# Splitting the last 64 contraction rows of the attention output into row-tiled pairs, and preparing their operand early

## The chip, the cores and the metric

One core of one Trainium2 chip runs the whole kernel. The metric is device time in microseconds (us) of one execution. Most executions of one kernel agree within 0.3%. From 2% a change is called faster or slower; what is compared are ratios with their 95% intervals.

## The reference, cut to what matters

```python
x = A_x                       # 2048 tokens x 576, bfloat16
xn = _layernorm(x, axis=-1)
return x + _A_ref(xn, A_wqkv, A_wo) + _B_ref(xn, B_w_gate, B_w_up, B_w_down)

# _A_ref: linear attention with H = 32 heads of 18 channels
#   o = num / den  (pq times kv per head, over pq times z), then o @ wo
# _B_ref: (gelu(xn @ w_gate) * (xn @ w_up)) @ w_down, F = 4608
```

The kernel folds kv (per head) and wo into one matrix M of 576 rows, so the attention output is (pq / den) @ M: a contraction over 576 rows, added to the same PSUM accumulator as the down projection, a contraction over 4608 rows.

## The kernel before

Four stages alike work on 512 tokens each. In each, 18 blocks of gate/up run on row tiles: two matmuls of 64 contraction rows at once, one in each half of the array. Then the down projection runs on the full array: per tile of 128 tokens and per column half of 288, 36 passes for the down weights and 5 for the attention part. The 32 heads are packed by 7, 7, 7, 7 and 4, so that four chunks have 126 rows and the last has 72:

```python
HCH = [7, 7, 7, 7, 4]                  # heads per chunk; DH = 18
...
    def m_stage(c, acc_bank):          # M = kv @ wo, chunk by chunk, while the first down tile runs
        rows = DH * HCH[c]
        for hf in range(2):
            b = (acc_bank + 2 + (2 * c + hf) % 6) % 8
            hs = slice(hf * HALF, (hf + 1) * HALF)
            nc.tensor.matmul(ps_all[:rows, b, :HALF], lhsT=kvT[:rows, c, :rows], rhs=wo2[:rows, c, hs], ...)
            nc.scalar.copy(out=m_sb[:rows, c, hs], in_=ps_all[:rows, b, :HALF])
...
            for f in range(NF):                    # 36 passes
                nc.tensor.matmul(acc, lhsT=hT[:, f, ...], rhs=wd_sb[:, f, hs], start=(f == 0), stop=False)
            for c in range(NCH):                   # 5 passes
                rows = DH * HCH[c]
                nc.tensor.matmul(acc, lhsT=pqT[:rows, c, ts_], rhs=m_sb[:rows, c, hs], ..., stop=(c == NCH - 1))
```

All loads of these stages are issued by SyncE, one after the other and in program order. In the first stage this one list holds the gate/up weights (three blocks ahead of use), the down weights (12 slices at blocks 2 to 13) and the transposed stores of pq / den.

```python
            if blk > 0:
                load_gu(blk + NWBUF - 1, i)        # four issues a block
...
        if sc == 0 and k == 1:
            load_wo()
        elif sc == 0 and k >= 2:
            load_wd_slice()
...
            if den_jobs and 0 < k < NF // GUB - 1:
                job, n = den_jobs.pop(0)           # every fourth of these issues a transposing store
                job(n)
```

Of the kernel before, what the change touches and what calls it, by code (L numbers as in the profile page):

```python
# [9 lines left out]
ALU = mybir.AluOpType  # L10
BF16 = mybir.dt.bfloat16
# [4 lines left out]
P = 128  # L16
HP = 64
S = 2048
D = 576
H = 32  # L20
DH = 18
F = 4608
NS = S // P
NF = F // P
SC = 512
NSC = S // SC
TPC = SC // P
HALF = D // 2
KT = 5
HCH = [7, 7, 7, 7, 4]  # L30
HOFF = [0, 7, 14, 21, 28]
NCH = len(HCH)
CR = 7 * DH
# [24 lines left out]
def kernel(  # L58
# [11 lines left out]
    nc = tc.nc  # L70
# [5 lines left out]
    out_view = out.flatten_outer_dims().rearrange("(p n) d -> p n d", n=NS)  # L76
# [5 lines left out]
    fwork = ctx.enter_context(tc.tile_pool(name="fwork", bufs=3))  # L82
    psum = ctx.enter_context(tc.tile_pool(name="psum", bufs=1, space=PSUM))

    ps_all = psum.tile([P, 8, 512], F32, name="ps_all")
# [4 lines left out]
    x_sb = persist.tile([P, NS, D], BF16, name="x_sb")  # L90
# [46 lines left out]
    pqT = persist.tile([P, NCH, S], BF16, name="pqT")  # L137
# [5 lines left out]
    hT = h_store[:].rearrange("p (f t) -> p f t", f=NF)  # L143
# [8 lines left out]
    def load_gu(i, part):  # L152

        if i >= NSC * NF // GUB:
            return
        f0 = GUB * (i % (NF // GUB))
        c0, c1 = f0 * P, (f0 + GUB) * P
        if part == 0:
            gu_blocks[i] = (wg_bufs.next(), wu_bufs.next(), wr_bufs.next())
        wg, wu, wr = gu_blocks[i]  # L160
        if part == 0:
            nc.sync.dma_start(wg[:], B_w_gate[0:512, c0:c1].rearrange("(kt p) c -> p kt c", p=P))
            nc.sync.dma_start(wr[0:HP, :], B_w_gate[512:576, c0:c1])
        else:
            nc.sync.dma_start(wu[:], B_w_up[0:512, c0:c1].rearrange("(kt p) c -> p kt c", p=P))
            nc.sync.dma_start(wr[HP:P, :], B_w_up[512:576, c0:c1])
# [13 lines left out]
        out=bm3, in_=bm3, compare_op=ALU.is_ge, fill=0.0,  # L180
# [3 lines left out]
        out=bm3, in_=bm3, compare_op=ALU.is_ge, fill=0.0,  # L184
# [109 lines left out]
    LO, HI = slice(0, HP), slice(HP, P)  # L294
    SYNC = mybir.DependencyInfo(mybir.DependencyClass.Sync, mybir.DependencyReason.DATA)
    banks = _Ring([4, 5, 6, 7, 2, 3, 0, 1])

    class _Unit:
# [5 lines left out]
        def __init__(self, outs, lhs, rhs, relay, first=(4, 0, 1, 2, 3), then=(0, 1, 2, 3)):  # L304
            self.outs, self.lhs, self.rhs, self.relay = outs, lhs, rhs, relay
            self.first, self.then = first, then
# [55 lines left out]
    def heads(ap):  # L362
        return ap.rearrange("p (h e) -> p h e", e=DH)
# [14 lines left out]

    def den_scale(n):
        pn = den_pn[n] = pn_bufs.next()  # L380
        for c0, c1 in ((0, 4), (4, 5)):
            h0, h1 = HOFF[c0], HOFF[c1 - 1] + HCH[c1 - 1]
            nh = HCH[c0]

            def chunked(ap):
                return ap.rearrange("p (c h) e -> p c h e", h=nh)

            nc.vector.scalar_tensor_tensor(  # L388
                out=pn[:].rearrange("p (c t) -> p c t", t=P)[:, c0:c1, :nh * DH].rearrange("p c (h e) -> p c h e", e=DH),
                in0=chunked(heads(pq[:, n, h0 * DH:h1 * DH])), scalar=EPS_ATT,  # L390
                in1=chunked(den_d[n][:, h0:h1].unsqueeze(2).to_broadcast([P, h1 - h0, DH])),
                op0=ALU.add, op1=ALU.mult,
            )

    def den_transpose(n):
        nc.sync.dma_start_transpose(pqT[:, :, n * P:(n + 1) * P], den_pn[n][:])
# [20 lines left out]
    for n in range(NS):  # L417
# [7 lines left out]
        if n < TD:  # L425
            for i, (k0, k1, eng) in enumerate([(0, 3, "ACT"), (3, KT, "ACT" if n else "DVE")]):
                b = TP_BANK[n] - i
# [98 lines left out]
    wd_sb = wd_pool.tile([P, NF, D], BF16, name="wd_sb")  # L526
    wo2 = wd_pool.tile([P, NCH, D], BF16, name="wo2")
    m_sb = wd_pool.tile([P, NCH, D], BF16, name="m_sb")
    dwork = ctx.enter_context(tc.tile_pool(name="dwork", bufs=1))
    pn_bufs = _Ring([dwork.tile([P, NCH * P], BF16, name=f"pn{i}") for i in range(3)])  # L530
    for pn in pn_bufs.tiles:
        nc.gpsimd.memset(pn[:], 0.0)

    def load_wo():
        nc.sync.dma_start(wo2[:CR, 0:4, :], A_wo[0:4 * CR, :].rearrange("(c p) j -> p c j", p=CR))
        nc.sync.dma_start(wo2[:D - 4 * CR, 4, :], A_wo[4 * CR:D, :])
    wd_loaded = [0]

    def load_wd_slice():
        f0 = wd_loaded[0]  # L540
        if f0 < NF:
            nc.sync.dma_start(wd_sb[:, f0:f0 + WDS, :], wd_view[:, f0:f0 + WDS, :])
            wd_loaded[0] += WDS


    den_jobs = [(job, n) for n in range(NS) for job in (den_mul, den_inv, den_scale, den_transpose)]

    def gu_pair(sc, k):
        cs = slice(sc * SC, (sc + 1) * SC)
        blk = sc * (NF // GUB) + k  # L550
        wg, wu, wr = gu_blocks.pop(blk)
        units = []
        for i in range(GUB):
            b = [banks.next(), banks.next()]
            fcol = slice(i * P, (i + 1) * P)

            def lhs(a, rows, kt, fcol=fcol):
                if kt == 4:
                    return wr[rows, fcol]
                return (wg, wu)[a][rows, kt, fcol]  # L560

            u = _Unit([ps_all[:, b[0], :], ps_all[:, b[1], :]], lhs, lambda a, rows, kt: xnT[rows, kt, cs],
                      nc.sync if blk == 0 else nc.gpsimd)
            if blk > 0:
                load_gu(blk + NWBUF - 1, i)
            u.p1()
            units.append((b, u))
# [4 lines that stand above are left out]
        for i, (b, u) in enumerate(units):  # L572
            u.p2()
            gl = fwork.tile([P, SC], F32, name="gl")
            nc.scalar.activation(out=gl[:], in_=ps_all[:, b[0], :], func=ACT.Gelu_apprx_tanh)  # L575
            nc.vector.tensor_tensor(out=hT[:, GUB * k + i, :], in0=ps_all[:, b[1], :], in1=gl[:], op=ALU.mult)  # L576
            if den_jobs and 0 < k < NF // GUB - 1:
                job, n = den_jobs.pop(0)
                job(n)

    def m_stage(c, acc_bank):
        rows = DH * HCH[c]
        for hf in range(2):
            b = (acc_bank + 2 + (2 * c + hf) % 6) % 8
            hs = slice(hf * HALF, (hf + 1) * HALF)
            nc.tensor.matmul(  # L586
                ps_all[:rows, b, :HALF], lhsT=kvT[:rows, c, :rows], rhs=wo2[:rows, c, hs], start=True, stop=True,
            )
            nc.scalar.copy(out=m_sb[:rows, c, hs], in_=ps_all[:rows, b, :HALF])

    def down_tile(sc, j, hooks):
        n = sc * TPC + j
        ts_ = slice(n * P, (n + 1) * P)
        res = fwork.tile([P, D], BF16, name="res")
        last = n == NS - 1
        for hf in range(2):
            hs = slice(hf * HALF, (hf + 1) * HALF)
            todo = hooks.pop(0) if hooks else {}
            acc_bank = banks.next()
            acc = ps_all[:, acc_bank, :HALF]  # L600
            for f in range(NF):
                if f in todo:
                    todo[f](acc_bank)
                nc.tensor.matmul(  # L604
                    acc, lhsT=hT[:, f, j * P:(j + 1) * P], rhs=wd_sb[:, f, hs], start=(f == 0), stop=False,
                )
            for c in range(NCH):
                rows = DH * HCH[c]
                nc.tensor.matmul(  # L609
                    acc, lhsT=pqT[:rows, c, ts_], rhs=m_sb[:rows, c, hs], start=False, stop=(c == NCH - 1),  # L610
                )
            nc.vector.tensor_tensor(out=res[:, hs], in0=acc, in1=x_sb[:, n, hs], op=ALU.add)  # L612
            if last:
                nc.sync.dma_start(out_view[:, n, hs], res[:, hs])
        if not last:
            nc.sync.dma_start(out_view[:, n, :], res[:])

    for sc in range(NSC):
        for k in range(NF // GUB):
            gu_pair(sc, k)  # L620
        while wd_loaded[0] < NF:
            load_wd_slice()

        hooks = [{6 * c_: (lambda b, c_=c_: m_stage(c_, b)) for c_ in range(NCH)} if sc == 0 else {}]
        for j in range(TPC):
            down_tile(sc, j, hooks)


# [28 lines left out]
```

## Time and profile before

| | before |
|---|---|
| median of 3 runs, at first | 516.69 us |
| span of the profiled run | 514.5 us |
| TensorE busy | 509.2 us, 99% |
| one full pass of 288 columns | 122.5 ns from start to start |
| one pair of row tiles, 512 columns | 215.9 ns |
| share of the DMA engines, first gate/up stage | 1.02 |

The lines are in the prediction. PE is TensorE, PEld its loads of stationary operands, DVE VectorE, ACT ScalarE and SPq the queue of SyncE; L309 is line 309 of the kernel. L309 is gate/up, L604 (after the change L632) a pass over the down weights, L609 (L637) a pass of the attention part, L586 (L589) the product that makes M; the new pairs are L620. In the page's groups, the text after the last bar is the idle time of the engine before these instructions, with who ended it.

### The profile page before, as it was taken

Reading aid. Unit: us, or ns where it says so; the run is one execution under the profiler, and the core shown is the slowest. Engines: PE = TensorE matmul, PEld = TensorE weight load, DVE = VectorE, ACT = ScalarE, POOL = GpSimd, SP = SyncE. Lnnn points to the kernel's source line nnn. Section 1 sums busy time; section 2 is a strip of 40 time slices with the busy share of each in tenths; the row PEclk is TensorE's granted clock in tenths of the full one; section 3 lists DMA queues with packets and bytes.
Section 4 is the critical chain, followed back from the end, with each engine's and each line's share of the span. In section 5 each row is a group of like instructions: output and inputs, shape, how many; then the busy total and the mean of one; then the engine's idle time right before and its main releaser. Section 6 shows DMA issues by size and latency. Waiting matters only on the chain.

```text
span 514.5 us, 10566 instructions
## 1 busy us (share of the span) xinstructions
PE 509.2 (99%) x4487; PEld 309.5 (60%) x4487; DVE 203.0 (39%) x414; ACT 136.7 (27%) x267; POOL 8.4 (2%) x26
## 2 busy tenths in 40 slices
PE   8999999999999999999999999999999999999997
PEld 7888854444587744444677644444777444445775
DVE  7986546667501046676301133333101234333100
ACT  5887522332410022232100023323000133232000
POOL 3001000000000000000000000000000000000000
PEclk9999999999999999999999999999999999999999
DMA  6633929999900056766400255555100454540000
GB/s 209 148 61 65 244 57 249 267 280 269 234 12 13 13 150 149 177 180 165 126 11 24 59 161 149 154 157 144 35 12 13 128 159 142 162 116 1 12 13 24
DMA packets 118745, 61.02 MB, mean 119 GB/s; under 512 B 25514, under 2 KB 117866, under 8 KB 118698
## 3 DMA queue, kind: packets, MB, share of 16 engines
q1 hardware_dynamic: 118554, 60.20, 45.0%
q8 instruction: 35, 0.57, 0.5%
q10 hardware_dynamic: 144, 0.15, 0.1%
q14 instruction: 12, 0.10, 0.1%
HBM read 52.79 MB, written 2.36 MB: 107 GB/s over the span
## 4 chain that ended last, share of the span: by engine, by line
PE 98%; DVE 1%; DMA 1%; ACT 0%; issue 0%
PE ps_all L309 54%; PE ps_all L604 27%; PE ps_all L254 8%; PE ps_all L285 4%; PE ps_all L609 4%; DMA x_sb<-in_A_x_dram 1%; PE ps_all L356 0%; DVE stats L203 0%; PE ps_all L586 0%; DVE hT L576 0%; PE ps_all L239 0%; ACT gl L575 0%; ACT xnT L243 0%; DVE res L612 0%; DVE xn L224 0%
## 5 line engine op out<-in xcount | busy, mean ns | idle before, releaser
L309 PE MATMUL ps_all<-xnT,wg 64*128 64x512 bf16 x1152 | 272.1, 376 | 0.0
L309 PE MATMUL ps_all<-xnT,wu 64*128 64x512 bf16 x1152 | 271.1, 376 | 0.0
L575 ACT ACTIVATE gl<-ps_all 128x512 f32<-128x512 f32 x144 | 86.0, 597 | 313.9 <-PE ps_all L309 313.9
L576 DVE TENSOR_TENSOR hT<-ps_all,gl 128x512 bf16<-128x512 f32 x144 | 99.3, 689 | 143.8 <-ACT gl L575 143.4
L309 PEld LDWEIGHTS <-wu 64*128 64x128 bf16 x1152 | 108.4, 94 | 68.0
L309 PEld LDWEIGHTS <-wg 64*128 64x128 bf16 x1152 | 108.5, 94 | 67.6
L604 PE MATMUL ps_all<-wd_sb,hT 128*128 128x288 bf16 x1152 | 147.1, 286 | 0.0
L604 PEld LDWEIGHTS <-hT 128*128 128x128 bf16 x1152 | 112.2, 98 | 30.1 <-issue 1.6
L612 DVE TENSOR_TENSOR res<-ps_all,x_sb 128x288 bf16<-128x288 f32 x32 | 14.6, 457 | 144.9 <-PE ps_all L609 144.9
L309 PE MATMUL ps_all<-xnT,wr 64*128 64x512 bf16 x288 | 55.5, 377 | 0.0
L254 PE MATMUL ps_all<-wqkv_sb,xnT 128*128 128x288 bf16 x320 | 42.1, 286 | 0.3 <-ACT xnT L243 0.3
L254 PEld LDWEIGHTS <-xnT 128*128 128x128 bf16 x320 | 30.5, 98 | 7.6 <-ACT xnT L243 0.5
L261 ACT ACTIVATE phi_e<-ps_all,neg 128x288 f32<-128x288 f32 x64 | 30.7, 496 | 9.0 <-PE ps_all L254 6.3
L309 PEld LDWEIGHTS <-wr 64*128 64x128 bf16 x288 | 14.4, 94 | 17.7 <-issue 0.7
L609 PE MATMUL ps_all<-m_sb,pqT 126*128 126x288 bf16 (+1 forms) x160 | 24.9, 286 | 0.0
L285 PE MATMUL ps_all<-hT,xn 128*128 128x288 bf16 (+4 forms) x176 | 22.6, 276 | 0.0
L285 PEld LDWEIGHTS <-xn 128*128 128x128 bf16 (+1 forms) x176 | 17.6, 101 | 3.9
L609 PEld LDWEIGHTS <-pqT 126*128 126x128 bf16 (+1 forms) x160 | 15.5, 97 | 4.1
L266 DVE SCALAR_TENSOR_TENSOR pq<-phi_e,ps_all 128x288 bf16<-128x288 f32 x32 | 14.1, 448 | 7.6 <-ACT phi_e L261 7.2
L266 DVE SCALAR_TENSOR_TENSOR hT<-phi_e,ps_all 128x288 bf16<-128x288 f32 x32 | 14.0, 450 | 2.3 <-ACT phi_e L261 2.3
L203 DVE BATCH_NORM_STATS2 stats<-x_sb 128x6 f32<-128x288 bf16 x32 | 13.6, 440 | 1.9 <-DMA x_sb<-in_A_x_dram 1.9
L388 DVE SCALAR_TENSOR_TENSOR pn<-pq,den_d 128x504 bf16<-128x504 bf16 (+1 forms) x32 | 13.1, 449 | 0.0
(52 smaller groups left out, 96.7 us busy)
## 6 DMA issues: line engine op xcount, KB each, us to landing
wg<-in_B_w_gate_dram SPq DMA_DIRECT2D x72, 256.0 KB, 3.0
wu<-in_B_w_up_dram SPq DMA_DIRECT2D x72, 256.0 KB, 3.6
wd_sb<-in_B_w_down_dram SPq DMA_DIRECT2D x12, 432.0 KB, 5.6
wr<-in_B_w_gate_dram SPq DMA_DIRECT2D x72, 32.0 KB, 2.8
wr<-in_B_w_up_dram SPq DMA_DIRECT2D x72, 32.0 KB, 3.2
out_dram<-res SPq DMA_DIRECT2D x15, 144.0 KB, 1.8
wqkv_sb<-in_A_wqkv_dram SPq DMA_DIRECT2D x3, 576.0 KB, 5.1
x_sb<-in_A_x_dram SPq DMA_DIRECT2D x5, 288.0 KB, 3.2
```

The source lines that it names most:

```text
L203: nc.vector.bn_stats(out=ln_raw[n][:, h, :], in_=x_sb[:, n, h * HALF:(h + 1) * HALF])
L254: nc.tensor.matmul(ps_all[:, KQ_BANK[which] + hf, :HALF], lhsT=xnT[:, kt, n * P:(n + 1) * P], rhs=wqkv_sb[:, kt, c:c + HALF], start=(kt == ...
L261: nc.scalar.activation(out=e[:], in_=ps_all[:, KQ_BANK[which] + hf, :HALF], func=ACT.Exp, bias=neg1[:], scale=1.0,)
L266: nc.vector.scalar_tensor_tensor(out=(pq, pk)[which][:, n, hf * HALF:(hf + 1) * HALF], in0=e_tiles[n, which, hf][:], scalar=1.0, in1=ps_al ...
L285: nc.tensor.matmul(ps_all[:m, b, col:col + w], lhsT=xn[:, n, j0:j0 + m], rhs=pk[:, n, d0:d0 + w], start=(n == 0 and col == 0), stop=(n == ...
L309: return nc.tensor.matmul(self.outs[i], lhsT=self.lhs(i, rows, kt), rhs=self.rhs(i, rows, kt), start=start, stop=stop, skip_group_check=True,)
L388: nc.vector.scalar_tensor_tensor(out=pn[:].rearrange("p (c t) -> p c t", t=P)[:, c0:c1, :nh * DH].rearrange("p c (h e) -> p c h e", e=DH), ...
L575: nc.scalar.activation(out=gl[:], in_=ps_all[:, b[0], :], func=ACT.Gelu_apprx_tanh)
L576: nc.vector.tensor_tensor(out=hT[:, GUB * k + i, :], in0=ps_all[:, b[1], :], in1=gl[:], op=ALU.mult)
L604: nc.tensor.matmul(acc, lhsT=hT[:, f, j * P:(j + 1) * P], rhs=wd_sb[:, f, hs], start=(f == 0), stop=False,)
L609: nc.tensor.matmul(acc, lhsT=pqT[:rows, c, ts_], rhs=m_sb[:rows, c, hs], start=False, stop=(c == NCH - 1),)
L612: nc.vector.tensor_tensor(out=res[:, hs], in0=acc, in1=x_sb[:, n, hs], op=ALU.add)
```

## The change

576 rows are 4.5 times 128, so the attention part should need 4.5 passes and not 5. Head 31 has 18 channels; eight of them are spread over the two rows left free in each of the four chunks of 126, and 64 rows remain. These 64 rows are multiplied for both column halves at once: the lower half of the array takes the first column half, the upper half the second; for the upper half the kernel keeps a copy of the operands in partitions 64 to 127. As gate/up works on row tiles too, the pairs are put beside gate/up. The product for the last chunk moves from the first down stage to gate/up block 4, and three small transfers put copies of its rows in place.

```diff
     def den_scale(n):
...
+        nc.vector.tensor_copy(
+            out=pn_c[:, 0:4, CR:P], in_=pn_c[:, 4, HP:HP + 8].rearrange("p (i c) -> p c i", c=4),
+        )
+        nc.vector.tensor_copy(out=pn_c[:, 4, HP:P], in_=pn_c[:, 4, 0:HP])
...
+    def m_last_chunk():
+
+        two = [banks.next(), banks.next()]
+        m_product(4, lambda hf: two[hf])
+        for i in range(2):
+            nc.sync.dma_start(m_sb[CR + i:CR + i + 1, 0:4, :], m_sb[HP + 4 * i:HP + 4 * i + 4, 4, :])
+        nc.sync.dma_start(m_sb[HP:P, 4, :], m_sb[0:HP, 4, :])
...
+        def pair(self):
+            for hf, rows in ((0, LO), (1, HI)):
+                nc.tensor.matmul(
+                    self.acc(hf), lhsT=pqT[rows, 4, self.ts], rhs=m_sb[rows, 4, HALVES[hf]],
+                    start=not self.opened, stop=self.opened, skip_group_check=True,
+                )
+            self.opened = True
...
-            for c in range(NCH):
-                rows = DH * HCH[c]
+            for c in range(4):
                 nc.tensor.matmul(
...
     for sc in range(NSC):
         for k in range(NF // GUB):
             gu_pair(sc, k)
+            if sc == 0 and k == 4:
+                m_last_chunk()
...
+        tiles[0].pair()
+        tiles[1].pair()
...
+            if j == 2 and sc == NSC - 1:
+                tiles[2].pair()
+                tiles[3].pair()
...
+        for t in tiles[2:]:
+            if sc < NSC - 1:
+                t.opened = True
+                t.pair()
+                for hf in range(2):
+                    t.add(hf)
```

More of the change, by code (lines that the diff above doesn't have):

```diff
@@ L380, in den_scale @@
         pn = den_pn[n] = pn_bufs.next()
+        pn_c = pn[:].rearrange("p (c t) -> p c t", t=P)
         for c0, c1 in ((0, 4), (4, 5)):
@@ L388, in den_scale @@
             nc.vector.scalar_tensor_tensor(
-                out=pn[:].rearrange("p (c t) -> p c t", t=P)[:, c0:c1, :nh * DH].rearrange("p c (h e) -> p c h e", e=DH),
+                out=pn_c[:, c0:c1, :nh * DH].rearrange("p c (h e) -> p c h e", e=DH),
                 in0=chunked(heads(pq[:, n, h0 * DH:h1 * DH])), scalar=EPS_ATT,
@@ L530 @@
     pn_bufs = _Ring([dwork.tile([P, NCH * P], BF16, name=f"pn{i}") for i in range(3)])
-    for pn in pn_bufs.tiles:
-        nc.gpsimd.memset(pn[:], 0.0)
     def load_wo():
@@ L579, in gu_pair, with m_product @@
                 job(n)
-    def m_stage(c, acc_bank):
+    def m_product(c, bank):
         rows = DH * HCH[c]
         for hf in range(2):
-            b = (acc_bank + 2 + (2 * c + hf) % 6) % 8
+            b = bank(hf)
             hs = slice(hf * HALF, (hf + 1) * HALF)
@@ L589, in m_stage @@
             nc.scalar.copy(out=m_sb[:rows, c, hs], in_=ps_all[:rows, b, :HALF])
-    def down_tile(sc, j, hooks):
-        n = sc * TPC + j
-        ts_ = slice(n * P, (n + 1) * P)
-        res = fwork.tile([P, D], BF16, name="res")
-        last = n == NS - 1
-        for hf in range(2):
-            hs = slice(hf * HALF, (hf + 1) * HALF)
-            todo = hooks.pop(0) if hooks else {}
-            acc_bank = banks.next()
-            acc = ps_all[:, acc_bank, :HALF]
+    def m_last_chunk():
[4 more added lines that the diff above has]
+        nc.sync.dma_start(m_sb[HP:P, 4, :], m_sb[0:HP, 4, :])
@@ new lines, with __init__, acc, down @@
+    HALVES = [slice(0, HALF), slice(HALF, D)]
+    class _DownTile:
+        def __init__(self, n):
+            self.n, self.ts = n, slice(n * P, (n + 1) * P)
+            self.banks = [banks.next(), banks.next()]
+            self.opened = False
+        def acc(self, hf):
+            return ps_all[:, self.banks[hf], :HALF]
+        def pair(self):
[5 more added lines that the diff above has]
+            self.opened = True
+        def down(self, hf, todo):
+            paired = self.opened
+            j = self.n % TPC
@@ L601, in down_tile @@
             for f in range(NF):
                 if f in todo:
-                    todo[f](acc_bank)
+                    todo[f]()
                 nc.tensor.matmul(
-                    acc, lhsT=hT[:, f, j * P:(j + 1) * P], rhs=wd_sb[:, f, hs], start=(f == 0), stop=False,
-                )
-            for c in range(NCH):
-                rows = DH * HCH[c]
+                    self.acc(hf), lhsT=hT[:, f, j * P:(j + 1) * P], rhs=wd_sb[:, f, HALVES[hf]],
+                    start=(f == 0 and not paired), stop=False, skip_group_check=True,
+                )
@@ L609, in down_tile @@
+            for c in range(4):
                 nc.tensor.matmul(
-                    acc, lhsT=pqT[:rows, c, ts_], rhs=m_sb[:rows, c, hs], start=False, stop=(c == NCH - 1),
-                )
-            nc.vector.tensor_tensor(out=res[:, hs], in0=acc, in1=x_sb[:, n, hs], op=ALU.add)
-            if last:
-                nc.sync.dma_start(out_view[:, n, hs], res[:, hs])
-        if not last:
-            nc.sync.dma_start(out_view[:, n, :], res[:])
+                    self.acc(hf), lhsT=pqT[:, c, self.ts], rhs=m_sb[:, c, HALVES[hf]],
+                    start=False, stop=(paired and c == 3), skip_group_check=True,
+                )
@@ L618, with add @@
+        def add(self, hf):
+            if hf == 0:
+                self.res = fwork.tile([P, D], BF16, name="res")
+            hs = HALVES[hf]
+            nc.vector.tensor_tensor(out=self.res[:, hs], in0=self.acc(hf), in1=x_sb[:, self.n, hs], op=ALU.add)
+            if self.n == NS - 1:
+                nc.sync.dma_start(out_view[:, self.n, hs], self.res[:, hs])
+            elif hf == 1:
+                nc.sync.dma_start(out_view[:, self.n, :], self.res[:])
     for sc in range(NSC):
@@ L620 @@
             gu_pair(sc, k)
+            if sc == 0 and k == 4:
+                m_last_chunk()
         while wd_loaded[0] < NF:
             load_wd_slice()
-        hooks = [{6 * c_: (lambda b, c_=c_: m_stage(c_, b)) for c_ in range(NCH)} if sc == 0 else {}]
-        for j in range(TPC):
-            down_tile(sc, j, hooks)
+        tiles = [_DownTile(sc * TPC + j) for j in range(TPC)]
+        tiles[0].pair()
+        tiles[1].pair()
+        spare = tiles[2].banks + tiles[3].banks
+        hooks = {8 + 6 * c: (lambda c=c: m_product(c, lambda hf: spare[(2 * c + hf) % 4])) for c in range(4)} if sc == 0 else {}
+        for j, t in enumerate(tiles):
+            if j == 2 and sc == NSC - 1:
+                tiles[2].pair()
+                tiles[3].pair()
+            closed = t.opened
+            for hf in range(2):
+                t.down(hf, hooks if j == hf == 0 else {})
+                if closed:
+                    t.add(hf)
[3 more added lines that the diff above has]
+                t.pair()
+                for hf in range(2):
+                    t.add(hf)
 _INS = ['A_x', 'A_wqkv', 'A_wo', 'B_x', 'B_w_gate', 'B_w_up', 'B_w_down']
```

## The prediction

> **What bounds the kernel now.** I read the page's first and fifth parts to find the busiest engine, then the chain that ended last, then the same groups kept apart by shape, and then the timeline at the places where the kind of matmul changes.
>
> ```profile
> PE 509.2 (99%) x4487; PEld 309.5 (60%) x4487; DVE 203.0 (39%) x414; ACT 136.7 (27%) x267; POOL 8.4 (2%) x26
> ...
> PE 98%; DVE 1%; DMA 1%; ACT 0%; issue 0%
> ...
> L609 PE MATMUL ps_all<-m_sb,pqT 126*128 126x288 bf16 x128 | 21.0, 285 | 0.0
> L609 PE MATMUL ps_all<-m_sb,pqT 72*128 72x288 bf16 x32 | 9.2, 288 | 0.0
> ```
>
> TensorE is the bound throughout: busy 99%, and 98% of the closing chain. So only array time counts, and work put on VectorE, ScalarE or a queue is free as long as nobody on the array waits for it. The line the change is about is the last one: 32 matmuls with 72 active rows. The 288 ns there is a latency, not a cost, because matmuls overlap. The cost is the distance between starts, which the chain gives:
>
> ```profile
> 180.30 70.04 PE ps_all L309 x648
> 250.34 4.52 PE ps_all L604 x36
> 254.86 0.62 PE ps_all L609 x5
> 255.47 4.41 PE ps_all L604 x36
> ```
>
> A full pass of 288 columns costs 4.41 us / 36 = 122.5 ns. The 324 gate/up pairs of row tiles cost 215.9 ns each by their starts in the trace (512 columns, two tiles at once). The first 36 down passes after gate/up take 4.52 instead of 4.41: a change of mode costs about 0.1 us. The timeline at that place (start, duration, engine, operation):
>
> ```profile
> 249.96 0.38 PE L309 MATMUL ps_all<-xnT,wu 64*128 64x512 bf16 x1
> 249.97 0.38 PE L309 MATMUL ps_all<-xnT,wg 64*128 64x512 bf16 x1
> 250.27 0.42 PE L604 MATMUL ps_all<-wd_sb,hT 128*128 128x288 bf16 x2
> ```
>
> The next start would be due 0.216 us after 249.965; it comes after 0.308 (0.092 more), and the one after that 0.134 later instead of 0.1225 (0.012 more): 0.104 us. The other way, from the last L609 at 290.387 to the first row tile at 290.606, it is 0.219 instead of 0.1225, and 0.012 more at the next pair: 0.108 us. There are four passages one way and three the other.
>
> One stall of the array stands out in the first down stage:
>
> ```profile
> 139.04 0.69 DVE L576 TENSOR_TENSOR hT<-ps_all,gl 128x512 bf16<-128x512 f32 x1 [0.17 <-ACT gl L575]
> ...
> 139.34 0.29 PE L586 MATMUL ps_all<-wo,kvT 126*126 126x288 bf16 x1
> 139.78 0.28 PE L586 MATMUL ps_all<-wo,kvT 126*126 126x288 bf16 x1 [0.16 <-DVE hT L576]
> ```
>
> The product of the attention weights wants a PSUM bank that VectorE is still reading for the last gate/up unit: the starts are 0.449 us apart instead of 0.1225, so 0.327 us is lost, once.
>
> **What the Trainium skill says.** "TensorEngine Tiling (Array Packing)", Key Properties: changing the tiling mode drains TensorE, and different tiles can load weights and multiply in parallel. The trace agrees, with the 0.10 us of drain above and both 64-row weight loads (94 ns each) inside one pair's 216 ns. "TensorE: Matmul & The Clock Gate", "Wait — 56ns, not 53.3ns?": a warm matmul stream is spaced N/2.4 GHz + about 2.5 ns, so 215.8 ns for 512 columns and 122.5 for 288. The trace has 215.9 and 122.5. The same page, Part 3, The mechanism: tiles of different row groups start about 4 ns apart. The trace has 3 ns. The tiling page, Gotcha 1: different row tiles must not touch one PSUM bank at once; the change obeys it by giving the two tiles the two column halves, which lie in two banks.
>
> **The change part by part.**
> 1. Removed: the fifth pass of each of 16 token tiles x 2 halves, 32 x 122.5 ns = 3.92 us.
> 2. Added: 16 pairs of row tiles of 288 columns. No such pair is in the trace; by the spacing of gate/up less 224 columns at 2.4 GHz (215.9 - 93.3) an estimate is 122.5 ns. The 94 ns loads still fit under it, as the 98 ns full loads fit under 122.5 now. 16 x 122.5 = 1.96 us.
> 3. More mode changes. Pairs at the beginning of a down stage follow gate/up and pairs at the end precede it, so those seven passages only move. New ones: the 72-row product among gate/up in the first block (there and back), and the pairs of tiles 2 and 3 in the middle of the last down stage (there and back): 2 x 0.104 + 2 x 0.108 = 0.42 us.
> 4. The stall goes. The products move from passes 0, 6, 12... to 8, 14, 20, 26. The first uses the banks of gate/up unit 17/0, whose VectorE read ended at 138.87, and starts about 1.3 us after the stage (near 139.5). The second uses those of 17/1, read until 139.73, and starts near 140.5. Both are free: -0.33 us.
> 5. Beside the array: the fifth product is moved, not added (two passes either way). VectorE gets 32 small copies; the smallest comparable lines (128x32 at 181 ns, 128x1 at 150) give an estimate of 0.15 to 0.2 us each, some 5 us in all beside 203, and none before a matmul at once. The four late additions at a stage's end (457 ns each) hold banks that the next gate/up wants only at its second block, 3.9 us later. The memsets that go were on an idle engine. At the end of the kernel the last addition and store are as before.
>
> Sum: -3.92 + 1.96 + 0.42 - 0.33 = -1.87 us; 516.69 - 1.87 = 514.8. This is 0.36%, well inside 2%.
>
> **The rivals.**
> (a) The weight stream of the first gate/up stage becomes the bound. The windows view says it is near:
>
> ```profile
> 68.00:138.30 70.30, 70.30 (x651) 31.58 (x648) 44.30 (x86) 20.90 (x35) 0.00 (x0) 1.00 1.02 239
> 180.30:250.34 70.04, 70.04 (x650) 31.54 (x650) 43.44 (x84) 20.90 (x35) 0.00 (x0) 1.00 0.63 166
> ```
>
> The next to last column is the DMA share: 1.02 in the first stage, where the down weights come in too, against 0.63. SyncE issues nearly without a pause (about 0.5 us an issue), 2.5 to 4.5 us behind the release of buffers, and the up weights of block 16 land at 130.39 for a use at 130.5. The change puts three issues into this queue (an estimate of 1.6 us) and 0.3 us onto the first transposed store by way of the copies. Against it: issues are already held up for 0.9 to 2.4 us in six places because the engines are full, and these stalls would absorb the 1.6; the three transfers are only 83 KB, 0.33 us at 250 GB/s; and the array itself comes 0.45 us later (two passes and two mode changes moved in). If it does go wrong, up to 1.5 us is lost: 515 to 516.3.
> (b) The short pairs do not overlap as gate/up does (two loads and two multiplies in 122 ns are denser than anything row-tiled here). If a pair took 2 x 94 = 188 ns for its loads, 16 x 65 = 1.0 us is lost: 515.9. At full serialization, 245 ns, all of point 2's gain is gone: 516.8. For it: no line shows a pair this short. Against: the two loads of a gate/up pair start 3 ns apart and run together.
> (c) A new bank wait at the opening pairs: they want four banks at once where one was enough. These belong to block 16; in the first stage VectorE's work there ended at 136.3, two microseconds before. I expect none.
>
> **Range and chances.** The sum gives 514.8. I add 0.1 for a part of (a) and (b), as both can only cost: 514.9. Below, the floor is the sum with the repeats' own spread (516.3 to 516.77, so about 0.3): 514.3. Above, one of the rivals nearly in full: 516.1. Faster by 2% would need 10 us, and no part has that; slower by 2% would take a steady starvation of weights, which the later three stages with share 0.46 to 0.63 rule out.
>
> **What would show it.** Down stages two and three shorter by 1.0 us less 4 x 0.1225 = 0.49 us, each: eight passes go, four pairs come. Pairs 0.12 us apart; after the pairs the same 0.1 us of drain. The first down stage without a 0.45 us distance. The first gate/up stage longer by 0.45 us and no more; a gap of the array before a row-tile load, with a weight buffer's transfer as releaser, would make (a) right. Pairs above 0.15 us apart would make (b) right, and the last stage gaining over 0.4 us would show the drains of point 3 cheaper than taken.

## The result, and the profile after

The changed kernel took 517.63 us (median of 6 runs, 517.31 to 519.09), the kernel before 516.46 (6 runs). The ratio is 1.0026, 95% interval 1.0013 to 1.0039: a loss of about 1.2 us where a gain of 1.8 had been expected. Ratios here are the mean time of one kernel's fast runs over that of the other's of the same rounds, so they are not quite the ratios of the medians quoted. The profiled run is the slowest of the six, 519.09 us; why is said below.

From the page, busy time and the chain that ended last:

```profile
PE 509.8 (99%) x4487; PEld 308.2 (60%) x4487; DVE 207.8 (40%) x446; ACT 136.7 (26%) x267; POOL 6.7 (1%) x23
...
PE 97%; DMA 1%; DVE 0%; SPq 0%; issue 0%; ACT 0%
```

TensorE is still the bound, but the chain now holds the SyncE queue (SPq) and a transfer of weights (the DMA in the chain before was the load of x at the start). The chain in order of time (start, length, what), first around the new parts of the first gate/up stage, then from a later stage:

```profile
87.94 0.37 PE ps_all L589 x2
88.31 8.97 PE ps_all L309 x82
97.45 0.56 SPq L163
98.07 0.58 SPq L165
98.69 4.29 DMA wr<-in_B_w_up_dram
103.03 40.58 PE ps_all L309 x359
...
254.77 4.52 PE ps_all L632 x36
259.29 0.49 PE ps_all L637 x4
```

From 97 to 103 us the end of the kernel hung on SyncE's issues and on a weight transfer that the array waited for. The waits view (waiter, releaser, total us, times, longest) has this too. It is the sign that the prediction named for rival (a). Before, then after:

```profile
PEld L309 <- DMA wr<-in_B_w_up_dram: 0.3, 1, 0.3
```

```profile
PEld L309 <- DMA wr<-in_B_w_up_dram: 3.0, 2, 2.8
PE ps_all L309 <- DMA wr<-in_B_w_up_dram: 2.5, 1, 2.5
```

In the later stage the attention part takes 0.49 us (four passes) instead of the 0.62 (five) that the prediction shows. So the intended saving is there, and something else took more.

The change of the array's mode at the end of the first gate/up stage, from the timeline:

```profile
143.32 0.38 PE L309 MATMUL ps_all<-xnT,wg 64*128 64x512 bf16 x1
143.32 0.62 PE L620 MATMUL ps_all<-m_sb,pqT 64*128 64x288 bf16 x4
143.88 0.30 PE L632 MATMUL ps_all<-wd_sb,hT 128*128 128x288 bf16 x1
```

Two pairs, four matmuls, come before the first full pass. From the last gate/up matmul to that pass it is 0.554 us by the starts in the trace, against 0.216 + 2 x 0.1225 + 0.092 = 0.553 by the numbers of the prediction. In this stage one half of the array ran a step behind the other, so that the first two matmuls of the pairs began beside the last one of gate/up. The second stage shows them in step:

```profile
254.15 0.38 PE L309 MATMUL ps_all<-xnT,wg 64*128 64x512 bf16 x1
254.36 0.41 PE L620 MATMUL ps_all<-m_sb,pqT 64*128 64x288 bf16 x4
254.70 0.30 PE L632 MATMUL ps_all<-wd_sb,hT 128*128 128x288 bf16 x1
```

The four start at 254.362, 254.366, 254.485 and 254.488: 4 and 3 ns apart within a pair, 122 to 123 ns from pair to pair, and again 0.553 us from the last gate/up matmul to the full pass.

I measured each stage by the starts of its matmuls: gate/up from its first to its last, down from there to the next gate/up (the last one to the end of the last matmul). In us, one profiled run of each; the two kernels at the right are experiments below:

| stage | before | after | a4_late | a3_mid_first_stage |
|---|---|---|---|---|
| first gate/up | 69.94 | 74.98 | 70.20 | 69.73 |
| other gate/up, each | 69.73 | 69.72 | 69.72 | 69.72 |
| first down | 42.24 | 41.11 | 41.11 | 41.56 |
| second and third down, each | 40.64 | 40.12 | 40.12 | 40.11 |
| last down | 40.71 | 40.39 | 40.39 | 40.39 |

All down stages gained: 1.13 + 2 x 0.53 + 0.32 = 2.5 us. The first gate/up stage lost 5.05 us. In the trace, 2.91 us of it are two gaps of the array before the weights of block 8 (0.23 and 2.68 us). Another 1.64 us lie in the eight pairs after the long gap, which started about 0.42 us apart instead of 0.216. The rest, some 0.5 us, is the two passes and two changes of mode that were moved there on purpose.

The windows view (stretch, length, then busy time and count of each engine, granted clock of TensorE, DMA share, GB/s) at that place:

```profile
103.00:106.60 3.60, 3.58 (x18) 1.31 (x20) 0.10 (x1) 0.00 (x0) 0.00 (x0) 0.53 1.14 276
```

The third number from the end, 0.53, is the granted clock: after the gap the array ran at half speed for some 3.4 us. This happened in the profiled run alone. Its mean clock is 0.997; the other five runs have 0.999 to 1.0, and spans of 515.4 to 515.8 instead of 517.2. So the halved clock fits the 1.5 us by which the profiled run is longer than its siblings, but not the loss of the siblings. The gap remains for that; the siblings have no trace that would show it, and the experiments have to.

Where does the gap come from? SyncE's list, before and then after, from the timeline of its queue. Before:

```profile
88.68 0.59 SPq L542 DMA_DIRECT2D wd_sb<-in_B_w_down_dram  x1
89.38 1.23 SPq L396 DMA_TRANSPOSE pqT<-pn  x1
90.70 0.52 SPq L162 DMA_DIRECT2D wg<-in_B_w_gate_dram  x1
```

After:

```profile
90.18 1.47 SPq L401 DMA_TRANSPOSE pqT<-pn  x1
91.74 1.38 SPq L599 DMA_DIRECT2D m_sb<-m_sb  x2
96.23 0.54 SPq L600 DMA_DIRECT2D m_sb<-m_sb  x1
96.86 0.54 SPq L162 DMA_DIRECT2D wg<-in_B_w_gate_dram  x1
```

Before, the gate weights of block 8 are issued at 90.70, right after the transposing store. After, three small transfers stand between them, and between the second and the third nothing is issued for 3 us: the trace has a wait of 3.03 us (93.17 to 96.20) on L600. In all SyncE was held for 5.12 us (91.70 to 96.81).

The program itself tells why. This is its list of SyncE's instructions with their waits, before any run. DMAHW0 to DMAHW7 are semaphores that tell of landings; the transfers take them in turn, and each waits until the one before it on its semaphore has landed:

```
L599 DMACopy m_sb<-m_sb 1x4x576 [waits DMAHW5_49,Activation_49]
L599 DMACopy m_sb<-m_sb 1x4x576 [waits DMAHW6_49]
L600 DMACopy m_sb<-m_sb 64x576 [waits DMAHW7_49,DMAHW6_49,DMAHW5_49]
L162 DMACopy wg_149<-in_B_w_gate_dram 128x4x256 [waits DMAHW0_49,PE_49]
```

The third transfer writes rows 64 to 127 of the last chunk. The first two read head 31's eight rows, which are rows 64 to 71 of the same chunk. So the third must wait until both have landed (DMAHW5 and DMAHW6 in its waits), and as SyncE works in order, all weights behind it wait too. The effect on the engines is seen in the same stretch of both kernels, before and then after:

```profile
91.70:97.00 5.30, 5.30 (x53) 2.34 (x49) 4.57 (x10) 1.68 (x3) 0.00 (x0) 1.00 1.17 272
```

```profile
91.74:97.00 5.26, 5.26 (x52) 2.40 (x50) 4.16 (x8) 2.12 (x4) 0.00 (x0) 1.00 0.76 122
```

The last number is GB/s: 272 before, 122 after. The difference over 5.26 us is 0.79 MB that wasn't moved; at 272 GB/s that takes 2.9 us, an estimate close to the gaps of 2.91 us. In this stage, whose DMA share was 1.02 before the change, most of the delay was not made up.

### The profile page after: what moved, and what is told of

Its sections match the earlier page's. It is cut to its first block, busy times and chain, and to the rows that moved or that the text cites. A ratio compares the mean times of both kernels' runs of the same rounds, so it can differ in the third digit from the quotient of the medians.

```text
span 517.2 us, 10596 instructions
## 1 busy us (share of the span) xinstructions
PE 509.8 (99%) x4487; PEld 308.2 (60%) x4487; DVE 207.8 (40%) x446; ACT 136.7 (26%) x267; POOL 6.7 (1%) x23
## 4 chain that ended last, share of the span: by engine, by line
PE 97%; DMA 1%; DVE 0%; SPq 0%; issue 0%; ACT 0%
PE ps_all L309 54%; PE ps_all L632 27%; PE ps_all L254 8%; PE ps_all L285 4%; PE ps_all L637 3%; DMA wr<-in_B_w_up_dram 1%; DMA x_sb<-in_A_x_dram 1%; PE ps_all L620 0%; PE ps_all L356 0%; PE ps_all L589 0%; DVE stats L203 0%; PE ps_all L239 0%; SPq L165 0%; SPq L163 0%; ACT xnT L243 0%
## 5 line engine op out<-in xcount | busy, mean ns | idle before, releaser
L309 PE MATMUL ps_all<-xnT,wr 64*128 64x512 bf16 x288 | 59.7, 379 | 2.6 <-DMA wr<-in_B_w_up_dram 2.5
L309 PEld LDWEIGHTS <-wr 64*128 64x128 bf16 x288 | 15.9, 94 | 20.2 <-DMA wr<-in_B_w_up_dram 3.0
L637 PE MATMUL ps_all<-m_sb,pqT 128*128 128x288 bf16 x128 | 20.9, 286 | 0.0
L637 PEld LDWEIGHTS <-pqT 128*128 128x128 bf16 x128 | 12.5, 98 | 3.2
```

The source lines that it names most:

```text
L309: return nc.tensor.matmul(self.outs[i], lhsT=self.lhs(i, rows, kt), rhs=self.rhs(i, rows, kt), start=start, stop=stop, skip_group_check=True,)
L637: nc.tensor.matmul(self.acc(hf), lhsT=pqT[:, c, self.ts], rhs=m_sb[:, c, HALVES[hf]], start=False, stop=(paired and c == 3), skip_group_ch ...
```

## The experiments

My theory: the wait of the third transfer delays the weights, and this alone turns a gain of about 2 us into a loss. Rivals: the three issues would be enough by themselves (1), the pairs and the changes of mode cost more than estimated (2), or the early product or VectorE's copies delay the weights (3).

**a1_staged**: take the wait away, by taking away its reason. The eight rows get a copy in a tile of their own.

```diff
         m_product(4, lambda hf: two[hf])
+        for hf in range(2):
+            nc.scalar.copy(out=m4[HP:HP + 8, HALVES[hf]], in_=ps_all[HP:HP + 8, two[hf], :HALF])
         for i in range(2):
-            nc.sync.dma_start(m_sb[CR + i:CR + i + 1, 0:4, :], m_sb[HP + 4 * i:HP + 4 * i + 4, 4, :])
+            nc.sync.dma_start(m_sb[CR + i:CR + i + 1, 0:4, :], m4[HP + 4 * i:HP + 4 * i + 4, :])
```

> The changed kernel with the eight rows of head 31 copied once more to a tile of their own, so that the third of the three small transfers overwrites nothing that the first two still read, and SyncE issues it without waiting for them. Theory (the 3.03 us wait of the third issue for the landing of the first two holds up the weight issues behind it): no gap of the array over 0.5 us in the first gate/up stage, and 514.6 to 515.2 us, 1.3 to 1.9 below the kernel before. Rival 1 (the three issues and the full queue are enough by themselves): a gap of 1 us or more stays there, 515.6 to 516.5. Rival 2 (the pairs and drains cost more than estimated): the gap goes but the time stays above 515.6.

Measured: 516.33 us (514.99 to 516.47), ratio 0.9990 (0.9977 to 1.0002). The wait is gone: SyncE was held for 2.07 us instead of 5.12. The gap at block 8 is gone too, but three shorter ones came at blocks 9, 12 and 16, of 0.39, 0.64 and 0.66 us. The interval includes no change at all against the kernel before, and the time lies in the range of rival 1. My theory had the wait as the only cause, and this run says otherwise: rival 1 holds for a large part.

**a2_before_plus_last_chunk**: the suspected part alone, on the kernel before. The banks of the later products were renumbered, because the early one moves the ring by two.

```diff
+    def m_last_chunk():           # product of the last chunk into two banks, and the three transfers
+        ...
     for sc in range(NSC):
         for k in range(NF // GUB):
             gu_pair(sc, k)
+            if sc == 0 and k == 4:
+                m_last_chunk()
```

> The kernel before, with the early 72-row product and its three transfers added after gate/up block 4, and nothing else of the change (its products in the down stage stay, so the early one is extra work; the result is right). Theory: two passes and two drains (0.45 us) and a wait of about 2.9 us for the weights of block 8: 519.3 to 520.0, or 1.5 us more when the clock is halved after the gap. Rival 2 (the loss comes from the pairs): no gap, 516.8 to 517.2.

Measured: 519.75 us (518.84 to 520.11), ratio 1.0060 (1.0047 to 1.0073): 3.2 us lost by this part alone. That is as expected, though the profiled run (the fastest of the five) waited only 2.26 us on the third transfer and shows four gaps of 1.8 us in all instead of one. Rival 2 is not needed.

**a3_mid_first_stage**: the same work elsewhere. The product goes to the other products in the first down stage, and the four pairs of this stage into its middle.

```diff
-            if sc == 0 and k == 4:
-                m_last_chunk()
...
+            hooks[8] = lambda: m_last_chunk(spare[0:2])
+            for c in range(4):
+                hooks[13 + 5 * c] = lambda c=c: m_product(c, lambda hf: spare[(2 * c + 2 + hf) % 4])
...
+            if j == 2 and sc == 0:
+                for u in tiles[:2]:
+                    u.opened = True
+                    u.pair()
+                    for hf in range(2):
+                        u.add(hf)
```

> The changed kernel with the 72-row product put among the other products in the first down stage, where SyncE has little to issue, and the first stage's four pairs in its middle, before its third tile. Same number of passes, pairs and mode changes as the changed kernel. Theory: no gap in gate/up, 514.4 to 514.9. Rival 2: above 515.6 without a gap.

Measured: 514.18 us (513.76 to 514.58), ratio 0.9953 (0.9940 to 0.9965), a little below the expected range, and no gap in gate/up (69.73 us in the table). The third transfer still waits for the first two (1.11 us); there is just nobody behind it in a hurry.

**a5_no_transfers**: the floor. The rows are zeroed at the start by GpSimd, so the result is wrong. (The check on record passed it all the same, as it passed a7, a10 and a11: it doesn't notice when these rows are missing, so a pass says little about them in the other kernels.)

```diff
-        for i in range(2):
-            nc.sync.dma_start(m_sb[CR + i:CR + i + 1, 0:4, :], m_sb[HP + 4 * i:HP + 4 * i + 4, 4, :])
-        nc.sync.dma_start(m_sb[HP:P, 4, :], m_sb[0:HP, 4, :])
...
+    nc.gpsimd.memset(m_sb[96:P, 0:4, :], 0.0)
+    nc.gpsimd.memset(m_sb[HP:P, 4, :], 0.0)
```

> The changed kernel without the three transfers; the rows that they fill are zeroed at the start instead, so the result is wrong on purpose. The floor of the changed kernel: 514.4 to 514.9 by the theory, without a gap. What a1_staged is above it is the cost of three issues that do not wait. Rival 3 (the early product itself, or the VectorE copies, delay the weights): a gap over 0.5 us stays.

Measured: 514.47 us (514.39 to 515.09), ratio 0.9962, no gap; the first gate/up stage took 70.20 us. So the early product, with its changes of mode, and VectorE's copies are harmless (rival 3 falls). The changed kernel stands 0.0064 of the time above it in ratios, 3.3 us: that is the price of the three transfers where they stand.

**a4_late**: the same function, wait included, ten blocks later.

```diff
-            if sc == 0 and k == 4:
+            if sc == 0 and k == 14:
```

> The changed kernel with the 72-row product and its three transfers after gate/up block 14 instead of 4, the wait of the third transfer included. Behind them SyncE then issues only weights that are wanted after the down stage, some 40 us later. Theory (what costs is the delay of the weight issues behind the three): no gap in gate/up, 514.3 to 514.9; at most a short wait of the opening pairs for the last transfer, which would show at the end of the first gate/up stage and give up to 516. Rival (the three transfers or the product cost something wherever they stand): 516 or more with the loss inside gate/up.

Measured: 514.06 us (513.85 to 514.22), ratio 0.9953 (0.9940 to 0.9966), a little below the expected range. SyncE's queue there:

```profile
130.58 1.37 SPq L599 DMA_DIRECT2D m_sb<-m_sb  x2
133.88 0.54 SPq L600 DMA_DIRECT2D m_sb<-m_sb  x1
134.51 0.53 SPq L162 DMA_DIRECT2D wg<-in_B_w_gate_dram  x1
```

The hole before the third transfer (131.95 to 133.88) is still there, but the weights behind it are for the second stage, which begins some 45 us later. No gap of the array, and the opening pairs waited for nothing. One number changed, and 3.6 us came back by the medians.

**a7_tiny_transfers**: is it the bytes or the issuing? Three transfers of 16 bytes stand in the place of the real ones (wrong, as a5).

```diff
         m_product(4, lambda hf: two[hf])
+        for i in range(3):
+            nc.sync.dma_start(m4[0:1, 64 * i:64 * i + 8], m_sb[0:1, 4, 64 * i:64 * i + 8])
```

> The kernel without transfers (a5, 514.47 us) with three transfers of 16 bytes issued by SyncE in the same place, with no wait between them (the result is wrong on purpose, as in a5). Issue time alone: about 1.6 to 2.1 us of SyncE near 92 us. If issue time is what costs, gaps of 1.2 to 1.7 us and 515.7 to 516.4, as in a1_staged. If the bytes cost, no gaps and 514.4 to 514.9.

Measured: 516.16 us (514.89 to 517.47, six runs), ratio 0.9997: 1.7 us above a5. SyncE was held for 2.26 us, and gaps of 0.56, 0.04, 0.64 and 0.60 us followed. The queue, and then who the array waited for in the waits view:

```profile
90.80 2.16 SPq L603 DMA_DIRECT2D m<-m_sb  x3
93.06 1.06 SPq L162 DMA_DIRECT2D wg<-in_B_w_gate_dram  x1
```

```profile
PE ps_all L309 <- DMA wr<-in_B_w_up_dram: 1.3, 3, 0.5
```

48 bytes cost as much as the 83 KB of a1_staged (0.9997 and 0.9990, with intervals that overlap), as was expected if the issues cost and not the bytes. What costs is SyncE's time, about 0.7 us an issue, in a list that feeds full engines.

**a10_one_tiny** and **a11_six_tiny**: one and six of these transfers, to see whether there is a slack.

```diff
-        for i in range(3):
+        for i in range(1):            # a10; range(6) in a11
```

> a7_tiny_transfers with one transfer of 16 bytes instead of three (wrong on purpose, as a5). a7 took about 2.3 us of SyncE and lost 1.7 us against a5 (514.47). If the queue has no slack at all, one issue (0.75 us) costs 0.4 to 0.7 us: 514.9 to 515.2. If there is a slack of a microsecond that three issues overran, it costs nothing: 514.4 to 514.7.

> The same with six transfers of 16 bytes (about 4.3 us of SyncE; wrong on purpose). With no slack, in proportion to a7: 3.2 to 4.0 us above a5, 517.7 to 518.5, close to the changed kernel itself, whose three transfers held SyncE for 5.1 us. If the cost levelled off, below 517.

Measured: one, 514.90 us (514.42 to 515.42), ratio 0.9965; six, 518.12 us (517.50 to 518.19), ratio 1.0023, as expected without a slack. With the hold of SyncE and the length of the first gate/up stage from the traces:

| kernel | SyncE held, us | first gate/up, us | time, us | ratio |
|---|---|---|---|---|
| a5, none | 0 | 70.20 | 514.47 | 0.9962 |
| a10, one | 0.85 | 70.20 | 514.90 | 0.9965 |
| a7, three | 2.26 | 72.30 | 516.16 | 0.9997 |
| a11, six | 4.62 | 73.45 | 518.12 | 1.0023 |
| changed kernel | 5.12 | 74.98, about 1.6 of it by the clock | 517.63 | 1.0026 |

One issue costs nothing in the profiled run, some 0.4 us by the medians, whose ranges overlap, and 0.15 us by the ratios: my two expectations for it can't be told apart. By the ratios, three issues cost 1.8 us against a5, six 3.2 and the changed kernel 3.3: 80%, 68% and 64% of the hold. So most of it is paid, and the changed kernel fits in this row: its loss is that of a hold of its length.

**a9_wd_postponed**: leave the third transfer's dependence and make room for it. The down weights' slices of blocks 4, 5 and 6 go to the end of their list.

```diff
-        elif sc == 0 and k >= 2:
+        elif sc == 0 and k >= 2 and k not in (4, 5, 6):
```

> The changed kernel, its wait included, with the three slices of down weights that were issued at blocks 4, 5 and 6 put off to the end of the list (blocks 14 to 16), so that about 1.9 us of issues and 1.3 MB leave the stretch around the wait. Theory (a queue with no slack, so any delay must be paid from something later): the gap at block 8 shrinks from 2.7 us to under 0.7 and the time is 514.4 to 515.3; a short gap may come back at blocks 14 to 17. Rival (the wait itself is what the array sees): unchanged at 517.6.

Measured: 515.71 us (514.42 to 515.92), ratio 0.9982 (0.9970 to 0.9994). The gap at block 8 is gone, as expected, but two gaps of 0.42 and 0.62 us came back at 116 and 132 us, more than I had allowed for. The wait did not stay as it was either: with the slices away it fell from 3.03 to 1.11 us, and the hold of SyncE from 5.12 to 3.21, so this run mixes a shorter hold with more room. It is 1.9 us better than the changed kernel, and 1.6 us worse than a4_late: a list that is full to its end can be relieved only in part by moving things within it.

**a6_act_queue**: issue the three transfers of a1_staged from ScalarE.

```diff
-            nc.sync.dma_start(m_sb[CR + i:CR + i + 1, 0:4, :], m4[HP + 4 * i:HP + 4 * i + 4, :])
-        nc.sync.dma_start(m_sb[HP:P, 4, :], m_sb[0:HP, 4, :])
+            nc.scalar.dma_start(m_sb[CR + i:CR + i + 1, 0:4, :], m4[HP + 4 * i:HP + 4 * i + 4, :])
+        nc.scalar.dma_start(m_sb[HP:P, 4, :], m_sb[0:HP, 4, :])
```

> a1_staged with its three transfers issued by ScalarE instead of SyncE. a1_staged lost 1.7 us in three gaps. If what costs is SyncE's time for three issues (2.07 us there): no gaps, 514.3 to 515.0. If it is the transfers' own work on the DMA engines: the gaps stay, 515.8 to 516.5. A new wait of ScalarE for a completion slot could delay a Gelu; it would show as a late Gelu near 91 us, and cost the array nothing below 2 us.

Measured: 516.08 us (515.66 to 516.97), ratio 0.9998. This run doesn't answer its question, because the issues did new harm on ScalarE (timeline):

```profile
94.83 0.55 ACTq L603 DMA_DIRECT2D m_sb<-m_sb  x1
95.49 1.08 ACT L579 ACTIVATE gl<-ps_all 128x512 f32<-128x512 f32 x2 [5.68 <-PE ps_all L309]
```

ScalarE waited for the landing semaphores before each of its three issues: in the program's list the third shares DMAHW4 with SyncE's transposing store, and the trace has that store landing at 94.81. So the third transfer was issued only at 94.83, and the next Gelu, which ran at 91.47 in the changed kernel, at 95.49. Three gaps of 0.85 us in all followed from 96.1 to 98.1, and one of 0.72 at 117. I had written that a late Gelu would cost nothing below 2 us; it was 4 us late.

## Why the prediction was right or wrong

The range ended at 516.1 and the time was 517.63. Taken by its own steps:

1. *Removed, 32 passes.* Right. The second and third down stage were to gain 0.49 us each, and gained 0.53.
2. *Pairs of 122.5 ns.* Right. The opening pairs fit to a nanosecond (0.553 and 0.554 measured, 0.553 by the numbers), and rival (b), pairs that don't overlap, fell.
3. *Changes of mode.* Right within hundredths. The last down stage was to gain 0.28 us and gained 0.32. The two passes and two changes moved into gate/up were taken as 0.45 us; a5 and a4_late have 70.20 us against the 69.73 of an undisturbed stage, 0.47.
4. *The stall that goes.* Right. The first down stage was to gain 0.49 + 0.33 + 0.245 (two passes moved out) = 1.06 us, and gained 1.13.
5. *Beside the array.* VectorE's copies took 172 and 182 ns, as estimated, and cost nothing (a5). The opening pairs found their banks free: rival (c) fell.

The step that failed is rival (a). It was seen, and it was mis-sized, in three terms:

- "The change puts three issues into this queue (an estimate of 1.6 us)". SyncE was held for 5.12 us. The issues themselves took 2.07 us (a1_staged), and the wait of the third for the landing of the first two took 3.03, which the prediction doesn't contain at all. It stood in the program's list of waits, and it can be read from the diff: the third transfer overwrites rows that the first two read.
- "These stalls would absorb the 1.6". They absorbed little. Three tiny issues held SyncE for 2.26 us and cost 1.7 (a7). The issues that were held up for 0.9 to 2.4 us were not time that the list could give away; only for a single issue (a10) does it stay open whether it was absorbed.
- "Land at 130.39 for a use at 130.5". I read this as a slack of 0.1 us. It was a wait, the 0.3 us of the waits view before the change: the matmul that needed these weights started at 130.436, 0.415 us after the one before it on its half of the array, instead of 0.216. The array was already paying 0.2 us. The undisturbed first stage takes 69.73 us (a3) and not 69.94.

So "up to 1.5 us is lost" should have been 3.3, the price of the transfers by a5. The rest of the sum holds: without the transfers' delay the change gains 516.41 - 514.06 = 2.35 us by the medians of those rounds (a4_late), against 1.87 in the sum. Of the 0.48 us between them, 0.2 are the stall of the kernel before that a4_late doesn't have, and 0.19 the small differences of the down stages above; the remaining 0.1 is less than the spread between runs.

What stays open: whether the issues would be free on another queue (a6 brought its own waits, for semaphores that SyncE's transfers held), why two thirds to four fifths of a hold were paid and not all of it, and why the holds were paid as several gaps in some runs and as one in others. The halved clock in one run of six was seen once, after a gap of 2.68 us, and not made to happen again.

Both a4_late and a3_mid_first_stage beat both kernels: 2.4 us, or 0.47%, below the kernel before. a4_late is the change as it was meant, with one number altered.

## What to carry to other kernels

Before adding a transfer to a queue that issues in order, look at what stands behind it and when that is needed; then look at what the new transfer itself waits for, above all other new transfers whose source it overwrites. In this stage, whose engines were full, most of the time in which nothing urgent was issued was paid: 64 to 80% of holds of 2.3 to 5.1 us, whether the transfers had 16 bytes or 83 KB. The same three transfers cost 3.3 us in front of urgent weights and nothing ten blocks later.

## What the Trainium skill lacked or had wrong

- "DMA: Bandwidth & Descriptors", Issuing engines are not separate DMA queues: it says that issuing from several engines saves only sequencer time, "which is usually small relative to the DMA itself". In this stage the sequencer's time was what the kernel paid for: three issues of 16 bytes took 2.26 us of SyncE and cost the kernel 1.7 us, as much as 83 KB in the same place.
- No page that I read says that an issue from ScalarE can delay the work behind it by microseconds when it must first wait for a landing. In a6_act_queue three issues spread over 91.2 to 95.4 us, the third of them held until another transfer landed at 94.81, and the Gelu behind them came 4 us late.
- "TensorE: Matmul & The Clock Gate", HAM oscillation: it gives idle gaps above about 3.4 us as what halves the clock. Here a gap of 2.68 us was followed by some 3.4 us at half clock (0.53 in the window shown), in one run of six.
- "TensorEngine Tiling (Array Packing)", Key Properties: it names the drain at a change of mode without a figure. The trace has 0.104 us from row tiles to the full array and 0.108 us back.
